# Splitting the second layer of the second chunk into float16 halves in a top-k attention and two-MLP kernel

## The chip, the cores and the metric

The kernel runs on one core of one Trainium2 chip. The metric is the time of one execution on the device in microseconds (us); lower is better. The median of three runs before the change is 1272.48 us.

## The reference, cut to what matters

```python
scores = q @ k.T / sqrt(64)                 # 4 batches, 8 heads, 576 x 576
attn   = softmax(where(scores >= 32nd largest of the row, scores, -1e9))
x = attn @ v                                # 2304 tokens x 512
x = (sigmoid(x @ w_gate) * (x @ w_val)) @ w_out          # 512 -> 1536 -> 512
out = relu(x @ w_in)**2 @ w_out2                         # 512 -> 2048 -> 512
```

The weights arrive as 64-bit numbers, q, k and v as float32.

## The kernel before, in words

Tokens are worked on in blocks of 128. The list `CHUNKS` (L28) makes them into twelve chunks: six of one block, then six of two. A chunk goes through attention first: for each of its blocks and each of eight heads one "unit" takes the scores (`sp`, TensorE), copies them to SBUF (`S`, ScalarE), finds the 32nd largest number of each row with four MAX8 and three MATCH_REPLACE (VectorE, L389 and L396), makes the softmax, transposes it and multiplies it with the values. Then the chunk goes through the first layer (gate, value, product, `w_out`) and the second (`w_in`, squared relu, `w_out2`). The weights are called `wg`, `wv`, `wo`, `wi` and `w2`; tiles of `w2` show as `w` in the profile.

There are two ways through the layers. `moe32` (L895) is the plain one, for the two chunks in `PLAIN` (L43): float32 weights (`wi_c` and so on, as converted from 64 bits) against float32 activations. A product of two float32 operands is two matmul instructions. `moe` (L768) is the split one, for all others: each weight is a pair of float16 tiles, a high half and what it leaves (`wi_w`), and so is each activation, and three matmuls (`SPLIT`) stand for one product. The split way needs power-of-two scales: of the weights (`scale`, L629, from a sum of squares on TensorE) and of each chunk's activations (L817 to L829: squares on ScalarE into `x`, their sum on TensorE into `x2pq`, its maximum on VectorE, `x2cm`, two halves on ScalarE and VectorE).

A weight is split by `split` (L653): a cast on ScalarE (L658) and a subtraction, on VectorE for two splits of three (L661) and on GpSimd for the third (`LOP`, L663 and L664). One split covers a pair of 128x512 blocks; there are 34 (6 each of wg, wv, wo, 8 each of wi, w2). A split writes a new tile and then frees the float32 one, so it comes behind the last plain use of that pair. In the kernel before, the main loop lists all splits in `todo` with the step of the second plain chunk at which each is due: a plain chunk has six steps of its first layer and eight of its second, so those of wg, wv and wo fall into its first layer and those of wi and w2 into its second.

Each layer works on two blocks of hidden columns at a time, a pair. In `moe32` one pair is in flight: the products of pair n+1 are issued ahead of the accumulation of pair n. In the split second layer three are (`DEPTH2`).

The program text gives each piece a priority (`at`, `tc.cur_priority`); a scheduler turns these into a fixed order of instructions on each engine. The weights come in over SyncE's queue with the queries, keys and values; SyncE also stores the outputs (`ob`).

Of the kernel before, what the change touches and what calls it, by code (L numbers as in the profile page):

```python
# [43 lines left out]
TD = 0  # L44
# [10 lines left out]
GRAM = {2: ("wg",), 3: ("wv",), 5: ("wo",), 9: ("wi",), 13: ("w2",)}  # L55
# [19 lines left out]
def tile_topk_attention__then__two_moe_layers(  # L75
# [692 lines left out]
    def moe(ci, nxt=None):  # L768

        m = ahead.pop(ci)  # L770
        tts, N, ix, l1_pair = chunks[ci], m.N, m.ix, m.l1_pair
        accs = []

        def l1_acc(fp, gh):
            if not accs:
                for h in range(2):
                    accs.append(ps_a.tile([P, 512], F32, tag="acc", name=f"acc1_{ci}_{h}"))

            last = fp == NF1 // 2 - 1
            for e, d in sorted(  # L780
                ((e, d) for e in range(2) for d in range(KM)),
                key=lambda t: (t[1], t[0]) if last else t,
            ):
                f = 2 * fp + e
                if True:
                    for x, (a, b_) in enumerate(SPLIT):
                        nc.tensor.matmul(  # L787
                            accs[d // 2][:, (d % 2) * N : (d % 2 + 1) * N],
                            wblk("wo", a, f, d * P, P),
                            gh[:, b_, e * N : (e + 1) * N],  # L790
                            start=(f == 0 and x == 0 and d % 2 == 0),
                            stop=(f == NF1 - 1 and x == 2),
                            skip_group_check=True,
                        )

        queue = m.queue
        depth = max(1, len(queue))
        for fp in range(len(queue), NF1 // 2):
            queue.append((fp, l1_pair(fp)))
            yield  # L800
            if len(queue) > depth:
                l1_acc(*queue.pop(0))
        while len(queue) > 1:
            l1_acc(*queue.pop(0))
        if nxt:
            nxt()
        l1_acc(*queue.pop(0))

        pool, kw = (wpool, {"tag": "w"}) if ci >= X2W else (mpool, {"tag": "m4", "bufs": M4})
        x2 = pool.tile([P, 2, KM, N], F16, name=f"x2_{ci}", **kw)  # L810
# [82 lines left out]


    def moe32(ci, xt):  # L895
# [387 lines left out]
```

## Time and profile before

| what | value |
|---|---|
| median of three runs (lowest to highest) | 1272.48 us (1272.18 to 1277.38) |
| the profiled execution: its time, its span | 1270.1 us, 1267.8 us |
| TensorE matmul busy | 1171.9 us, 92% of the span |
| VectorE, ScalarE, GpSimd busy | 956.3, 830.0, 844.9 us (75%, 65%, 67%) |
| chain that ended last | TensorE 62%, VectorE 14%, ScalarE 9%, DMA 7%, GpSimd 5% |

The span runs from the first to the last instruction of the profiled execution; its time includes what lies around it. A matmul's record lasts longer than the step from one to the next, since matmuls overlap; the pace is read from the chain, which merges those that follow each other. In the rows below PE is TensorE, PEld its weight loads, DVE VectorE, ACT ScalarE, POOL GpSimd and SPq SyncE's queue.

### The profile page before, as it was taken

The page shows a single profiled execution, that of the slowest core. Times are in us where ns is not written, and L with a number is a line of the kernel's source. Part 1 is how long each engine was busy: PE and PEld are TensorE (multiplying, and loading weights), DVE is VectorE, ACT ScalarE, POOL GpSimd, SP SyncE. Part 2 cuts the span into 40 slices and gives each one's busy share as a digit, 9 for nine tenths or more (in the row PEclk, how much of TensorE's full clock was granted, in tenths as well). Part 3 has the DMA queues.
Part 4 walks back from the last instruction along what each step waited for, and adds up shares of the span by engine and source line. Part 5 has one row for each costly group of instructions (what it writes and reads, how often), then busy time and mean ns, then how long its engine had stood idle before and what let it go on. Part 6 is the DMA issues. An engine that isn't in the chain of part 4 may idle for free.

```text
span 1267.8 us, 30670 instructions
## 1 busy us (share of the span) xinstructions
PE 1171.9 (92%) x11477; PEld 952.5 (75%) x11477; DVE 956.3 (75%) x1965; ACT 830.0 (65%) x1719; POOL 844.9 (67%) x1294
## 2 busy tenths in 40 slices
PE   6657889999889989899998999999999999999998
PEld 5436877987777868779786778877886887787775
DVE  6998789899789868889997788998999969210010
ACT  4998996577676766667766676776676757322122
POOL 1788774488776576777875887797688749515223
PEclk9667999999989999999997999999999999999999
DMA  6988763223354346665667465466544623200000
GB/s 183 366 293 284 259 191 85 57 78 88 109 151 118 95 93 147 147 134 119 146 128 155 99 164 120 119 138 154 105 101 92 126 48 67 55 1 1 18 1 17
DMA packets 243188, 153.92 MB, mean 121 GB/s; under 512 B 193120, under 2 KB 209504, under 8 KB 243040
## 3 DMA queue, kind: packets, MB, share of 16 engines
q1 hardware_dynamic: 243040, 151.97, 47.1%
q8 instruction: 90, 1.47, 0.5%
q14 instruction: 58, 0.48, 0.1%
HBM read 105.51 MB, written 18.09 MB: 97 GB/s over the span
## 4 chain that ended last, share of the span: by engine, by line
PE 62%; DVE 14%; ACT 9%; DMA 7%; POOL 5%; issue 3%; SPq 1%; DVEq 0%; POOLq 0%; ACTq 0%
PE ph L851 11%; PE acc L872 10%; PE pv L747 7%; PE pg L747 7%; PE acc L787 6%; PE sp L374 6%; DVE mx L389 5%; DVE W L396 5%; PE xp L506 2%; PE ph L952 2%; DMA PT<-S 2%; DMA kst<-ks 2%; PE acc L969 2%; PE xp L533 2%; PE qpt L334 1%
## 5 line engine op out<-in xcount | busy, mean ns | idle before, releaser
L389 DVE MAX8 mx<-W 128x8 f32<-128x576 f32 x432 | 327.9, 759 | 11.1
L396 DVE MATCH_REPLACE8 W<-mx,W 128x576 f32<-128x576 f32 x288 | 213.8, 742 | 0.0
L851 PE MATMUL ph<-x,wi_w 128*128 128x256 f16 (+1 forms) x1920 | 190.7, 252 | 4.6 <-ACT x L825 3.6
L872 PE MATMUL acc<-w_w,rh 128*128 128x512 f16 x768 | 181.8, 379 | 2.2 <-POOL rh L864 2.2
L851 PEld LDWEIGHTS <-wi_w 128*128 128x128 f16 x1920 | 156.4, 98 | 30.6 <-issue 5.2
L747 PE MATMUL pv<-xs,wv_w 128*128 128x256 f16 (+1 forms) x1440 | 147.0, 254 | 6.0 <-DVE th L759 4.8
L747 PE MATMUL pg<-xs,wg_w 128*128 128x256 f16 (+1 forms) x1440 | 148.2, 253 | 3.1 <-ACT xs L520 2.2
L374 PE MATMUL sp<-kst,qt 128*128 128x288 f32 x608 | 135.3, 335 | 15.7 <-DMA kst<-ks 8.8
L408 ACT ACTIVATE W<-S,mx 128x576 f32<-128x576 f32 x144 | 111.8, 776 | 51.7 <-DVE mx L389 51.4
L454 POOL TENSOR_TENSOR S<-W,S 128x512 f16<-128x512 f32 x192 | 137.0, 736 | 1.6
L747 PEld LDWEIGHTS <-wv_w 128*128 128x128 f16 x1440 | 117.9, 99 | 22.1 <-issue 9.2
L747 PEld LDWEIGHTS <-wg_w 128*128 128x128 f16 x1440 | 118.6, 99 | 17.4 <-issue 1.0
L377 ACT COPY S<-sp 128x576 f32<-128x576 f32 x144 | 92.0, 639 | 57.3 <-PE sp L374 37.5
L872 PEld LDWEIGHTS <-rh 128*128 128x128 f16 x768 | 72.5, 98 | 74.0 <-POOL rh L864 2.8
L787 PEld LDWEIGHTS <-wo_w 128*128 128x128 f16 x1440 | 117.9, 98 | 12.6 <-issue 0.8
L389 DVE MAX8 mx<-S 128x8 f32<-128x576 f32 x144 | 107.3, 745 | 25.0 <-ACT S L377 25.0
L759 DVE TENSOR_TENSOR th<-pv,th 128x512 f32<-128x512 f32 (+1 forms) x60 | 34.5, 576 | 121.3 <-PE pv L747 113.9
L374 PEld LDWEIGHTS sp<-kst,qt 128*128 128x128 f32 x608 | 92.4, 196 | 27.8 <-DMA kst<-ks 8.0
L452 POOL TENSOR_SCALAR W<-W,rz 128x576 f32<-128x576 f32 x96 | 71.9, 749 | 59.8 <-ACT S L451 57.4
L863 POOL TENSOR_TENSOR r<-r 128x512 f32<-128x512 f32 (+1 forms) x80 | 69.6, 871 | 57.4 <-ACT rh L862 51.8
L451 ACT ACTIVATE S<-W,rz 128x576 f16<-128x576 f32 x96 | 74.2, 774 | 50.4 <-DVE rz L447 47.1
L396 DVE MATCH_REPLACE8 W<-mx,S 128x576 f32<-128x576 f32 x144 | 106.9, 743 | 0.3 <-issue 0.3
(290 smaller groups left out, 2349.6 us busy)
## 6 DMA issues: line engine op xcount, KB each, us to landing
kst<-ks SPq DMA_DIRECT2D x112, 288.0 KB, 3.2
v<-vd SPq DMA_DIRECT2D x32, 320.0 KB, 3.4
qn<-in_q_dram SPq DMA_DIRECT2D x128, 64.0 KB, 2.4
wi_r<-in_moe_w_in_dram SPq DMA_DIRECT2D x16, 512.0 KB, 6.1
w_r<-in_moe_w_out_dram SPq DMA_DIRECT2D x16, 512.0 KB, 4.5
v<-in_v_dram SPq DMA_DIRECT2D x56, 128.0 KB, 2.4
wg_r<-in_moe_w_gate_dram SPq DMA_DIRECT2D x12, 512.0 KB, 6.4
wv_r<-in_moe_w_val_dram SPq DMA_DIRECT2D x12, 512.0 KB, 7.0
```

Of the source, the lines that this page charges most:

```text
L374: nc.tensor.matmul(sp[:, e, 0:HALF], l, r, start=(x == 0), stop=(x == len(ops) - 1))
L377: nc.scalar.copy(ss.rearrange("p (e s) -> p e s", e=2), sp[:, :, 0:HALF])
L389: m8 = nc.vector.max(mx[:, r], cur)
L396: nc.vector.match_replace(wk, mx[:, r], cur, NEG)
L408: nc.scalar.activation(wk, ss, AF.Prelu, bias=kth, scale=-1.0, alpha=1.0 / BIG)
L451: nc.scalar.activation(pp[:, 0:S], wk, AF.Copy, scale=rz)
L452: nc.gpsimd.tensor_scalar(wk, wk, rz, 1.0, op0=ALU.mult, op1=ALU.mult)
L454: nc.gpsimd.tensor_tensor(pp[:, o : o + e - f], wk[:, f:e], pp[:, f:e], op=ALU.subtract)
L747: nc.tensor.matmul(pp[:, e * N : (e + 1) * N], wblk(wd, a, c, f0, P), xs[:, b_, c, :], start=(e == 0 and n == 0), stop=(n == 3 * KM - 1), ...
L787: nc.tensor.matmul(accs[d // 2][:, (d % 2) * N : (d % 2 + 1) * N], wblk("wo", a, f, d * P, P), gh[:, b_, e * N : (e + 1) * N], start=(f == ...
L851: nc.tensor.matmul(ph[:, e * N : (e + 1) * N], wblk("wi", a, c, f0, P), x2[:, b_, c, :], start=(e == 0 and n == 0), stop=(n == 3 * KM - 1) ...
L872: nc.tensor.matmul(acc2[i][:, 0:DM], gh[:, b_, e * N + i * P : e * N + (i + 1) * P], wblk("w2", a, f, 0, DM), start=(f == 0 and x == 0), s ...
```

## The change

The second chunk keeps the plain first layer and takes the split second layer. For that the second half of `moe` becomes a function `second`, which both `moe` and `moe32` call; the second chunk's split activations are written over its own input tile. The splits of wi and w2 are due while the first chunk does its second layer (as soon as all weights have been converted), those of wg, wv and wo in the second chunk's first layer as before. The scales of wi and w2 are taken two steps earlier. The first chunk's plain second layer holds two pairs in flight. Intermediate results of the plain layers are written in place instead of to a second buffer. The second chunk's second layer gets steps of 3 instead of 4 in the priority count.

```diff
-TD = 0
+MIXED = (1,)
+DEPTH1 = (1, 1)
+DEPTHP = 2
+CMS = 3.0
+W2S = 12
...
-GRAM = {2: ("wg",), 3: ("wv",), 5: ("wo",), 9: ("wi",), 13: ("w2",)}
+GRAM = {2: ("wg",), 3: ("wv",), 5: ("wo",), 7: ("wi",), 11: ("w2",)}
...
+    def second(ci, ix, x2, srcs, nxt=None):
...
+        if ix is None:
+
+            nc.vector.scalar_tensor_tensor(
+                us[:, 0:1], iy, float(2.0 ** (2 * TB - 7)), scales["wi"][1], op0=ALU.mult, op1=ALU.mult
+            )
...
+        yield from second(ci, ix, x2, srcs, nxt)
...
-            g = mpool.tile([P, 2 * N], F32, tag="hi", bufs=HIB, name=f"g_{ci}_{fp}")
-            nc.vector.tensor_tensor(g, pg[:, 2 * N : 4 * N], th, op=ALU.mult)
-            return g
+            nc.vector.tensor_tensor(th, pg[:, 2 * N : 4 * N], th, op=ALU.mult)
+            return th
...
+        if ci in MIXED:
+            x2 = xt.rearrange("p d n -> p (d n)").bitcast(F16)
+            h = KM * N // 2
+            yield from second(
+                ci,
+                None,
+                x2.rearrange("p (a c n) -> p a c n", a=2, c=KM),
+                [accs[0][:, i * h : (i + 1) * h].rearrange("p (d n) -> p d n", d=KM // 2) for i in range(2)],
+            )
+            return
...
-            if prev is not None:
-                l2_acc(*prev)
-            prev = (fp, g)
-        l2_acc(*prev)
+            if len(prev) > DEPTHP:
+                l2_acc(*prev.pop(0))
+        for p in prev:
+            l2_acc(*p)
...
+    ends = {n: (len(PLAIN) - 1) * per_chunk for n in ("wg", "wv", "wo")}
+    ends.update({n: (len(PLAIN) - 1 - len(MIXED)) * per_chunk for n in ("wi", "w2")})
...
-        todo.append((n1 + 2 * (i // 2) + 2, "wi", i))
+        todo.append((ends["wi"] + n1 + 2 * (i // 2) + 2, "wi", i))
...
-        todo.append((n1 + i + 3, "w2", i))
-    todo = [(max(t[0], TD), *t[1:]) for t in todo]
+        todo.append((ends["w2"] + max(n1 + i + 2 + DEPTHP, W2S), "w2", i))
...
-                tm += CM
-                if ci == PLAIN[-1]:
+                tm += CM if ci not in MIXED or n <= n1 else CMS
+                if nstep[0] == len(steps):
                     at(tm - SUP)
-                    while todo and todo[0][0] <= n:
+                    while todo and todo[0][0] <= PLAIN.index(ci) * per_chunk + n:
                         split(*todo.pop(0)[1:])
```

The scheduler's order moves with it. Three places follow; a name's first numbers are chunk or block, then head or pair, and the last one only counts tiles.

VectorE late in the first chunk's second layer, softmax of block 2, heads 4 and 5. Before:

```order
L389 MAX mx_2_4_2490<-W_2_4_2489 128x8
L396 MATCH_REPLACE W_2_4_2489<-mx_2_4_2490,W_2_4_2489 128x576
L389 MAX mx_2_4_2490<-W_2_4_2489 128x8
L389 MAX mx_2_5_2568<-S_2_5_2452 128x8
L396 MATCH_REPLACE W_2_5_2567<-mx_2_5_2568,S_2_5_2452 128x576
L389 MAX mx_2_5_2568<-W_2_5_2567 128x8
```

Changed:

```order
L393 MAX mx_2_4_2521<-W_2_4_2520 128x8
L665 SCALAR_TENSOR_TENSOR w2_w0_2254<-w2_c0_1659,w2s_2230,w2_w0_2254 128x1024
L400 MATCH_REPLACE W_2_4_2520<-mx_2_4_2521,W_2_4_2520 128x576
L665 SCALAR_TENSOR_TENSOR w2_w1_2257<-w2_c1_1673,w2s_2230,w2_w1_2257 128x1024
L393 MAX mx_2_4_2521<-W_2_4_2520 128x8
L393 MAX mx_2_5_2602<-S_2_5_2483 128x8
L665 SCALAR_TENSOR_TENSOR w2_w3_2321<-w2_c3_1701,w2s_2230,w2_w3_2321 128x1024
L400 MATCH_REPLACE W_2_5_2601<-mx_2_5_2602,S_2_5_2483 128x576
L665 SCALAR_TENSOR_TENSOR wi_w6_2396<-wi_c6_1631,wis_1930,wi_w6_2396 128x1024
L393 MAX mx_2_5_2602<-W_2_5_2601 128x8
```

Splits of w2 and wi now stand between the steps of the softmax, where there were none.

TensorE between the two layers of the second chunk (`acc1_1` ends its first layer, `ph_1_0` begins its second). Before:

```order
L927 MATMUL acc1_1_2585<-g_1_5_2827,wo_c5_1036 128x128 x8
L374 MATMUL sp_3_4_3109<-kst_3_4_0_3021,qt_3_2_0_3033 128x288
L474 MATMUL tp_3_1_3038<-ident_81,W_3_1_2980 128x128 x4
L492 MATMUL tq_3_0_3045<-ident_81,we_3_0_2918 128x128
L374 MATMUL sp_3_4_3109<-kst_3_4_0_3021,qt_3_2_0_3033 128x288 x3
L952 MATMUL ph_1_0_2939<-x_plain_269,wi_c0_1072 128x128 x2
```

Changed, from the last matmul of the new sum of squares on:

```order
L783 MATMUL x2pq_1_2970<-x_plain_269,ones_86 128x128
L338 MATMUL qpt_3_2_3144<-ident_81,qn_3_2_3027 128x128 x2
L378 MATMUL sp_3_4_3241<-kst_3_4_0_3135,qt_3_2_0_3147 128x288 x4
L478 MATMUL tp_3_1_3152<-ident_81,W_3_1_3052 128x128 x4
L496 MATMUL tq_3_0_3159<-ident_81,we_3_0_2951 128x128
L823 LDWEIGHTS wi_w0_1945
L823 MATMUL ph_1_0_2992<-x_plain_269,wi_w0_1945 128x128
```

The same attention work stands between the layers, with the queries' transposes (`qpt`) more; the sum of squares stands ahead of it, and behind it come weight loads and matmuls of the split `wi`.

VectorE in the third chunk's first layer, softmax of block 4, head 1. Before:

```order
L389 MAX mx_4_1_3721<-W_4_1_3720 128x8
L661 SCALAR_TENSOR_TENSOR w2_w3_3263<-w2_c3_1707,w2s_2361,w2_w3_3263 128x1024
L396 MATCH_REPLACE W_4_1_3720<-mx_4_1_3721,W_4_1_3720 128x576
L389 MAX mx_4_1_3721<-W_4_1_3720 128x8
L661 SCALAR_TENSOR_TENSOR w2_w4_3330<-w2_c4_1719,w2s_2361,w2_w4_3330 128x1024
L396 MATCH_REPLACE W_4_1_3720<-mx_4_1_3721,W_4_1_3720 128x576
L759 TENSOR_TENSOR th_2_2_3970<-pv_2_2_3921,th_2_2_3970 128x256
L389 MAX mx_4_1_3721<-W_4_1_3720 128x8
```

Changed:

```order
L393 MAX mx_4_1_3897<-W_4_1_3896 128x8
L400 MATCH_REPLACE W_4_1_3896<-mx_4_1_3897,W_4_1_3896 128x576
L393 MAX mx_4_1_3897<-W_4_1_3896 128x8
L763 TENSOR_TENSOR th_2_2_4146<-pv_2_2_4097,th_2_2_4146 128x256
L400 MATCH_REPLACE W_4_1_3896<-mx_4_1_3897,W_4_1_3896 128x576
L393 MAX mx_4_1_3897<-W_4_1_3896 128x8
```

The splits that stood ahead of `th_2_2` have gone.

## Rows read from the trace of the kernel before

**Rows 1.** Table of stretches: window, each engine's busy us, TensorE's granted clock, DMA share, GB/s.

```profile
core 0: us, PE busy (x) PEld busy (x) DVE busy (x) ACT busy (x) POOL busy (x), PEclk, DMA share, GB/s
175.00:277.50 102.50, 100.45 (x873) 86.99 (x873) 92.91 (x182) 69.88 (x135) 58.04 (x84) 1.00 0.31 86
277.50:329.00 51.50, 50.52 (x422) 39.97 (x421) 43.78 (x79) 42.45 (x89) 41.74 (x61) 1.00 0.38 109
329.00:363.70 34.70, 27.78 (x422) 26.57 (x419) 29.70 (x58) 23.40 (x53) 26.76 (x41) 0.95 0.36 100
...
450.00:550.00 100.00, 88.99 (x1232) 74.16 (x1230) 75.28 (x172) 65.85 (x162) 75.98 (x139) 1.00 0.57 127
...
700.00:1060.00 360.00, 356.74 (x3457) 282.97 (x3456) 320.43 (x664) 248.04 (x517) 279.56 (x457) 1.00 0.52 114
```

**Rows 2.** Chain of waits, second chunk's plain second layer: start, length, what.

```profile
283.64 1.78 PE ph L952 x16
285.43 1.72 PE acc L969 x4
```

**Rows 3.** Chain of waits, third chunk's split second layer.

```profile
372.16 1.56 PE ph L851 x28
...
378.98 1.29 PE acc L872 x6
```

**Rows 4.** Timeline of TensorE between the third chunk's layers: start, length; idle before.

```profile
362.71 0.27 PE L819 MATMUL x2pq<-x,ones 128*128 128x128 bf16 x2 [1.74 <-ACT x L817]
...
364.24 1.62 PE L374 MATMUL sp<-kst,qt 128*128 128x288 f32 x7 [0.97 <-POOL qt L350]
366.59 0.85 PE L374 MATMUL sp<-kst,qt 128*128 128x288 f32 x2 [0.73 <-ACT S L377]
367.24 1.93 PE L851 MATMUL ph<-x,wi_w 128*128 128x128 f16 x16
```

**Rows 5.** Timeline of TensorE between the fourth chunk's layers.

```profile
443.73 0.40 PE L819 MATMUL x2pq<-x,ones 128*128 128x128 bf16 x4
...
447.36 1.28 PE L851 MATMUL ph<-x,wi_w 128*128 128x128 f16 x20 [1.12 <-ACT x L825]
```

**Rows 6.** Timeline of SyncE's queue: the store of the second chunk's output.

```profile
319.23 0.34 SPq L988 DMA_DIRECT2D out_dram<-ob  x1
```

**Rows 7.** Groups of instructions, 175 to 365 us, ScalarE and GpSimd: busy us, mean ns, idle before.

```profile
L658 ACT ACTIVATE wi_w<-wi_c,wis 128x1024 f16<-128x1024 f32 x8 | 9.2, 1151 | 1.9 <-DVE w_w L661 1.9
...
L664 POOL TENSOR_TENSOR wi_w<-wi_c,wi_w 128x1024 f16<-128x1024 f32 x2 | 4.3, 2132 | 0.0
...
L663 POOL TENSOR_SCALAR wi_c<-wi_c,wis 128x1024 f32<-128x1024 f32 x2 | 2.2, 1122 | 2.0 <-ACT wi_w L658 2.0
```

**Rows 8.** Groups of instructions, 175 to 365 us, VectorE: splits of w2 and wi.

```profile
L661 DVE SCALAR_TENSOR_TENSOR w_w<-w_c,w2s,w_w 128x1024 f16<-128x1024 f32 x5 | 10.1, 2020 | 0.9 <-ACT w_w L658 0.9
...
L661 DVE SCALAR_TENSOR_TENSOR wi_w<-wi_c,wis,wi_w 128x1024 f16<-128x1024 f32 x6 | 8.6, 1435 | 0.1
```

**Rows 9.** Timeline of VectorE in the third chunk's first layer.

```profile
332.85 4.37 DVE L661 SCALAR_TENSOR_TENSOR w_w<-w_c,w2s,w_w 128x1024 f16<-128x1024 f32 x1
...
340.57 0.42 DVE L759 TENSOR_TENSOR th<-pv,th 128x256 f32<-128x256 f32 x1
```

**Rows 10.** Costliest groups of the page, VectorE's softmax steps: busy us, mean ns, idle before.

```profile
L389 DVE MAX8 mx<-W 128x8 f32<-128x576 f32 x432 | 327.9, 759 | 11.1
L396 DVE MATCH_REPLACE8 W<-mx,W 128x576 f32<-128x576 f32 x288 | 213.8, 742 | 0.0
```

**Rows 11.** Timeline of TensorE in the third chunk's first layer.

```profile
334.78 1.50 PE L747 MATMUL pg<-xs,wg_w 128*128 128x128 f16 x24
341.04 2.57 PE L747 MATMUL pv<-xs,wv_w 128*128 128x128 f16 x24 [4.75 <-DVE th L759]
```

**Rows 12.** Timeline of GpSimd there, the first and last of seven in a row.

```profile
331.41 0.70 POOL L225 TENSOR_SCALAR vm<-vm,vsc 128x512 f32<-128x512 f32 x1
...
334.98 1.15 POOL L711 TENSOR_TENSOR xs<-xt,xs 128x512 f16<-128x512 f32 x1
```

**Rows 13.** Table of stretches, right behind TensorE's wait.

```profile
341.10:343.40 2.30, 2.30 (x24) 2.30 (x24) 2.23 (x5) 1.89 (x8) 2.12 (x4) 0.53 0.11 35
```

More of the change, by code (lines that the diff above doesn't have):

```diff
@@ L766, in moe_head @@
         m.N, m.ix, m.l1_pair = N, ix, l1_pair
[L768 to L810, printed above, removed]
+    def second(ci, ix, x2, srcs, nxt=None):
+        tts = chunks[ci]
+        N = len(tts) * P
         KH = KM // 2
-        srcs = [a[:, 0 : KH * N].rearrange("p (d n) -> p d n", d=KH) for a in accs]
         with tc.high_priority(offset=XUP):
@@ L892, in moe, with l1_acc @@
         yield
+    def moe(ci, nxt=None):
+        m = ahead.pop(ci)
+        tts, N, ix, l1_pair = chunks[ci], m.N, m.ix, m.l1_pair
+        accs = []
+        def l1_acc(fp, gh):
+            if not accs:
+                for h in range(2):
+                    accs.append(ps_a.tile([P, 512], F32, tag="acc", name=f"acc1_{ci}_{h}"))
+            last = fp == NF1 // 2 - 1
+            for e, d in sorted(
+                ((e, d) for e in range(2) for d in range(KM)),
+                key=lambda t: (t[1], t[0]) if last else t,
+            ):
+                f = 2 * fp + e
+                if True:
+                    for x, (a, b_) in enumerate(SPLIT):
+                        nc.tensor.matmul(
+                            accs[d // 2][:, (d % 2) * N : (d % 2 + 1) * N],
+                            wblk("wo", a, f, d * P, P),
+                            gh[:, b_, e * N : (e + 1) * N],
+                            start=(f == 0 and x == 0 and d % 2 == 0),
+                            stop=(f == NF1 - 1 and x == 2),
+                            skip_group_check=True,
+                        )
+        queue = m.queue
+        depth = max(1, len(queue))
+        for fp in range(len(queue), NF1 // 2):
+            queue.append((fp, l1_pair(fp)))
+            yield
+            if len(queue) > depth:
+                l1_acc(*queue.pop(0))
+        while len(queue) > 1:
+            l1_acc(*queue.pop(0))
+        if nxt:
+            nxt()
+        l1_acc(*queue.pop(0))
+        pool, kw = (wpool, {"tag": "w"}) if ci >= X2W else (mpool, {"tag": "m4", "bufs": M4})
+        x2 = pool.tile([P, 2, KM, N], F16, name=f"x2_{ci}", **kw)
+        KH = KM // 2
+        srcs = [a[:, 0 : KH * N].rearrange("p (d n) -> p d n", d=KH) for a in accs]
+        yield from second(ci, ix, x2, srcs, nxt)
     def moe32(ci, xt):
@@ L961, in l2_pair @@
             nc.scalar.activation(r, ph[:, 0 : 2 * N], AF.Relu)
-            g = mpool.tile([P, 2 * N], F32, tag="hi", bufs=HIB, name=f"rr_{ci}_{fp}")
-            nc.gpsimd.tensor_tensor(g, r, r, op=ALU.mult)
-            return g
+            nc.gpsimd.tensor_tensor(r, r, r, op=ALU.mult)
+            return r
         def l2_acc(fp, g):
@@ L975, in l2_acc @@
                 )
-        prev = None
+        prev = []
         for fp in range(NF2 // 2):
-            g = l2_pair(fp)
+            prev.append((fp, l2_pair(fp)))
             yield
-            if prev is not None:
-                l2_acc(*prev)
-            prev = (fp, g)
-        l2_acc(*prev)
+            if len(prev) > DEPTHP:
+                l2_acc(*prev.pop(0))
+        for p in prev:
+            l2_acc(*p)
         tt = chunks[ci][0]
@@ L1149, in layer2_scales @@
             usc.append(u)
-        return usc[0], scales["w2"][1]
+        return usc[0]
     att = attention()
```

22 lines of the change are left out of this document (13 added, 9 removed).

## The prediction, made before the change was run

> **What bounds the kernel now.** I read the table of stretches first, then the timelines inside them, then the chain of waits for the pace of single operations. The edits act between 175 us, where the first chunk turns from its first to its second layer, and 363.7 us, where the third chunk does; the stretches are cut at the places where the second chunk does so (277.5 us) and where the third has done two pairs (329 us). The reader is to see three different limits [rows 1]. In stage A (175 to 277.5) TensorE is busy 100.45 of 102.50 us and VectorE 92.91: TensorE is full, but VectorE has only 9.6 us to spare. In stage B (277.5 to 329) TensorE is busy 50.52 of 51.50, VectorE 43.78: TensorE alone. In stage C (329 to 363.7) neither is full: TensorE 27.78 of 34.70. Later TensorE leaves 11 of 100 us free between 450 and 550 us, and 3.3 of 360 between 700 and 1060: from there on it runs almost without a gap, so microseconds won before stay won unless the 450 to 550 us stretch eats them.
>
> **Second layer of the second chunk (stage B).** Removed are 128 float32 matmuls of 128 columns and 32 of 512 (two instructions for each of 64 and 16 products). In the chain 16 of the first kind took 1.78 us and 4 of the second 1.72 [rows 2], so 111 ns and 430 ns each: 14.2 + 13.8 = 28.0 us. Added are 192 float16 matmuls of 128 columns and 48 of 512. The third chunk runs the same ones now: 28 took 1.56 us and 6 took 1.29 [rows 3], so 56 and 215 ns: 10.7 + 10.3 = 21.0, with four of the norm (56 ns each, 0.2) 21.2. **TensorE saves 6.8 us**, on the path, since stage B is TensorE's.
>
> Against that stands a new wait. The plain second layer only copied its input; the split one must square it, sum it on TensorE, find a power of two on VectorE, and write two halves. The third chunk shows this at the same width: from the first matmul of the sum at 362.71 to the first product at 367.24 us, with waits of 1.74, 0.97 and 0.73 us in and ahead of it [rows 4], 3.4 us idle. The fourth chunk shows it better covered: from 443.73 to 447.36 with 1.12 us idle [rows 5]. In the new order the queries, scores and a transpose of the attention stand between the sum and the first product, as in the third chunk, so I take 2.5 us, between ends of 1.1 and 3.4. **Stage B: -6.8 + 2.5 = -4.3 us.**
>
> The other engines there: per pair ScalarE gets a square and GpSimd a subtraction more, eight times, work that the third chunk hides today; their splits leave the stage. On SyncE's queue the store of the second chunk's output moves ahead of three key loads of later units that used to stand ahead of it. It is one issue of 0.34 us [rows 6], but if the output is late, those loads stand behind it. I cost it at nothing, since the layer that ends in it is shorter.
>
> **The splits go to stage A.** Each of the 34 splits is one ScalarE cast, 1.15 us, and a subtraction, on VectorE for two of three and on GpSimd for the third (2.13 us after a scaling of 1.12) [rows 7]. The order now has 20 VectorE splits ahead of the second chunk's second layer where it had 10, then three in stage B (it had eight) and none in stage C (it had five). Half a unit of softmax less stands ahead of that point (26.5 units instead of 27). The price of a VectorE split is uncertain: the six of wi took 1.435 us in the mean, the five of w2 2.02, a single one of them 4.37 [rows 8, 9]. Without that one these eleven come to (6 x 1.435 + 5 x 2.02 - 4.37) / 10 = 1.43 us. Ten more cost 14.3; half a unit (two MAX8 of 0.76, one and a half MATCH_REPLACE of 0.74 [rows 10]) gives 2.6 back. That is 11.7 us against 9.6 us of spare VectorE. **Stage A: +2.1 us.** If enough of it slips in beside full TensorE it is 0; at 2.02 us a split with all the spare time used it is +8.0. ScalarE gets 15 more casts (17.3 us on 69.88 of 102.5 busy) and GpSimd five more pairs (16.3 on 58.04) [rows 1]: both still fit.
>
> **Stage C loses its stall.** TensorE stood idle for 4.75 us ahead of 341.04, for VectorE's `th` of the pair before [rows 11]. VectorE was late because the split of w2 that began at 332.85 took 4.37 us [rows 9], while GpSimd ran without a pause from 331.41 to 336.1 [rows 12]. With no split left here that goes. After the stall the granted clock was 0.53 of full, about the lower level of 1.2 GHz [rows 13], and the next 24 matmuls took 2.57 us where 24 had taken 1.50 before it [rows 11]: another 1.1. What is late next is the norm of the third chunk (its 3.4 us stay). **Stage C: -4.75 - 1.1 = -5.9 us.**
>
> The Trainium skill ("SBUF — State Buffer", section "SBUF: two separate sides") says that a VectorE instruction with two SBUF inputs and a GpSimd instruction that reads SBUF take a shared port pair in turn, each for its whole length. The 4.37 us beside GpSimd's run agrees. The page speaks against this change: in stage A GpSimd goes from 58 to 74 us of work, and more splits would meet it. By the splits' row without the long one the sum stays what it is below; by the page, with every new split meeting GpSimd, it would be that of rival 2.
>
> **Two pairs in flight, one buffer instead of two.** In the first chunk's plain second layer TensorE has no idle time worth a row (stage A is full at 100.45 of 102.50). I cost the deeper queue and the in-place writes at nothing; what hides the latency is the attention's matmuls. Wherever VectorE makes those late, the extra pair is what TensorE has left. The scales of wi and w2 come one and two units of softmax earlier, same work.
>
> **Sum.** +2.1 - 4.3 - 5.9 = -8.1 us. The profiled execution took 1270.1 us, so it would take 1262.0; the median of the runs shown is 1272.48, 2.4 higher, so the forecast is **1264.4 us**. At 363.7 us both orders have done the same number of softmax units, and the work behind it is the same, so I add nothing. The ends: A 0, B -5.7, C -5.9 gives 1260.9; A +8.0, B -3.4, C -4.75 gives 1272.3.
>
> **Rivals.**
> (1) VectorE starves TensorE in stage A: none of the 9.6 us of spare time can be used, because VectorE's idle moments come from waiting for scores. Then A is +11.7, the sum +1.5, the time 1274. For it: two engines at 98 and 91% in one stage. Against it: in stage A the old order already used such moments for ten splits.
> (2) The slower side: the same, with every one of the ten new splits held up by GpSimd as the w2 splits were, 2.02 us each. A is then 20.2 - 2.6 = +17.6, the sum +7.4, the time 1279.9. It is slower by over 0.5% from 1.92 us a split on, if no spare time is used. For it: GpSimd's third of the splits moves to the same place, and GpSimd's subtraction takes 2.13 us, longer than a free split. Against it: between them GpSimd was idle for 44 of 102.5 us. The rule of the page above is the mechanism of this rival.
> (3) The gain is given back between 450 and 550 us, where transfers and VectorE already leave TensorE idle for 11 us [rows 1]: half of it gone is 1268.5. Against it: those waits hang on earlier engine work, which comes earlier too.
> (4) The change doesn't do what it says: the split layer doesn't run at 56 ns a matmul because each wait leaves TensorE at the low clock. 24 matmuls in 2.57 us are 107 ns; a fifth of the layer at that pace with the full wait of 3.4 is some 3 us less gain, 1267.
> (5) Better: the third chunk's norm wait also shrinks by 3.4 us with ScalarE freed of splits, and A costs nothing: 1264.4 - 2.1 - 3.4 = 1258.9 or a little less.
>
> **How the numbers follow.** Forecast with its own range of 1260 to 1268: 0.56. Rival 1: 0.12; 2: 0.09; 3: 0.12; 4: 0.05; 5: 0.06. A measurement of this kernel tells about 0.5% from no change, so faster means below 1266.1 and slower above 1278.8. Faster: most of the forecast (0.48) and rival 5: 0.54. Slower: the larger part of rival 2, 0.07. The rest, 0.39, is within. The range of 1257 to 1274 leaves out rival 2, part of rival 1 and a little beyond rival 5.
>
> **What would show it.** Right: the float16 second layer of the second chunk within some 21 us of TensorE's own time; no VectorE split after the second chunk's second layer has begun but three; no wait of TensorE above 2 us in the third chunk's first layer; the second chunk's second layer beginning within a few microseconds of 277.5. Wrong: TensorE idle for transposes or scores before 277 us (rivals 1 and 2, told apart by the mean of VectorE's splits there); a longer 450 to 550 us stretch (3); low granted clock in the split layer (4).

## The result: 1282.3 us, slower

The changed kernel takes **1282.32 us** in the median (1279.54 to 1283.14), the kernel before 1273.76 beside it: ratio **1.0065, interval 1.0048 to 1.0082**, so 0.65% more. The forecast was 1264.4, with a range of 1257 to 1274. Rival 2 (VectorE's splits held up by GpSimd) had 1279.9.

The profiled execution of the changed kernel took 1283.14 us (span 1281.4). Its table of stretches, to be read beside [rows 1]; the second chunk's norm is at 288.4 us now (before, its second layer began at 277.5), the third chunk's at 368.7 (363.7):

```profile
core 0: us, PE busy (x) PEld busy (x) DVE busy (x) ACT busy (x) POOL busy (x), PEclk, DMA share, GB/s
175.00:222.00 47.00, 45.06 (x402) 36.74 (x403) 44.43 (x89) 36.25 (x71) 28.98 (x40) 1.00 0.43 120
222.00:255.00 33.00, 25.42 (x177) 21.83 (x177) 30.43 (x41) 23.61 (x36) 30.91 (x27) 0.90 0.18 53
255.00:288.40 33.40, 32.14 (x293) 30.16 (x291) 31.87 (x54) 26.14 (x46) 25.84 (x27) 1.00 0.23 62
175.00:288.40 113.40, 102.62 (x868) 88.73 (x868) 106.73 (x182) 86.00 (x151) 85.73 (x94) 0.97 0.30 83
288.40:339.00 50.60, 46.35 (x517) 37.09 (x518) 42.37 (x92) 36.27 (x92) 33.73 (x63) 0.97 0.35 96
339.00:368.70 29.70, 26.33 (x408) 24.61 (x406) 19.03 (x50) 16.22 (x41) 17.69 (x36) 1.00 0.45 125
...
368.70:1281.40 912.70, 871.98 (x8965) 697.68 (x8964) 646.88 (x1391) 545.39 (x1178) 597.03 (x990) 0.99 0.43 98
```

Stage A takes 113.4 us instead of 102.5 (+10.9), B and C together 80.3 instead of 86.2 (-5.9). TensorE's idle time in A is 10.8 us (2.0 before). Most of the loss sits in one third of A, from 222 to 255 us: TensorE busy 25.42 of 33 at a clock of 0.90, and GpSimd, which the prediction counted as having room, busy 30.91 (16.64 in the same window before). In A as a whole GpSimd has 85.73 us instead of 58.04.

The wait itself, on TensorE, and behind it the second chunk's norm:

```profile
249.90 3.79 PE L945 MATMUL acc<-th,wo_c 128*128 128x128 f32 x16 [7.29 <-DVE th L935]
...
283.84 2.05 PE L945 MATMUL acc<-th,wo_c 128*128 128x128 f32 x16
...
287.24 0.55 PE L783 MATMUL x2pq<-x_plain,ones 128*128 128x128 bf16 x4 [0.67 <-ACT x_plain L781]
...
290.07 0.40 PE L378 MATMUL sp<-kst,qt 128*128 128x288 f32 x1 [1.76 <-ACT qt L350]
291.59 0.66 PE L378 MATMUL sp<-kst,qt 128*128 128x288 f32 x3 [1.12 <-POOL qt L354]
292.70 1.12 PE L478 MATMUL tp<-ident,W 128*128 128x128 f32 x4 [0.45 <-POOL W L442]
```

After 7.29 us of idling the granted clock is 0.50, the lower level of 1.2 GHz (249.90 to 253.50 us), and the next 16 float32 matmuls take 3.79 us where 16 of the same take 2.05 later (283.84): another 1.7 us. Why `th` was late stands in the timelines of VectorE, GpSimd and ScalarE (start, length, what, idle before):

```profile
243.88 1.90 DVE L665 SCALAR_TENSOR_TENSOR wv_w<-wv_c,wvs,wv_w 128x1024 f16<-128x1024 f32 x1 [1.92 <-ACT wv_w L662]
...
246.44 3.06 DVE L665 SCALAR_TENSOR_TENSOR wg_w<-wg_c,wgs,wg_w 128x1024 f16<-128x1024 f32 x1
249.43 0.41 DVE L935 TENSOR_TENSOR th<-pg,th 128x256 f32<-128x256 f32 x1
```

```profile
235.02 2.14 POOL L668 TENSOR_TENSOR w_w<-w_c,w_w 128x1024 f16<-128x1024 f32 x1
237.14 2.15 POOL L667 TENSOR_SCALAR wi_c<-wi_c,wis 128x1024 f32<-128x1024 f32 x1
239.38 1.06 POOL L432 TENSOR_SCALAR bs<-bs 128x1 f32<-128x1 f32 x1
240.53 2.14 POOL L668 TENSOR_TENSOR wi_w<-wi_c,wi_w 128x1024 f16<-128x1024 f32 x1
...
244.69 1.27 POOL L409 TENSOR_SCALAR bs<-mx 128x1 f32<-128x1 f32 x1
245.93 0.40 POOL L934 TENSOR_SCALAR th<-th 128x256 f32<-128x256 f32 x1
246.30 2.12 POOL L668 TENSOR_TENSOR wg_w<-wg_c,wg_w 128x1024 f16<-128x1024 f32 x1
```

```profile
242.70 1.15 ACT L662 ACTIVATE wv_w<-wv_c,wvs 128x1024 f16<-128x1024 f32 x1 [2.62 <-POOL wi_w L668]
...
244.22 0.39 ACT L933 ACTIVATE th<-pg 128x256 f32<-128x256 f32 x1
```

Read it backwards. VectorE's `th` (249.43) stood behind a split that took 3.06 us and ended 1.08 us after GpSimd's own subtraction (246.30 to 248.42); the shortest splits of the stage take 1.26. GpSimd had made its part of that `th` ready at 246.33, behind an instruction on a single column (`bs`, 128x1) that took 1.27 us. ScalarE's part (244.22) and the split before (243.88) stood behind a cast that, by the trace, waited until 242.70 for GpSimd's subtraction of wi. From 231 to 254 us GpSimd had no pause above 0.1 us; its subtraction of wi had followed on a scaling of 2.15 us, instead of the 1.12 of [rows 7], and on another single column of 1.06.

### The profile page after: what moved, and what is told of

Its sections match the earlier page's. It is cut to its first block, busy times and chain, and to the rows that moved or that the text cites. A ratio compares the mean times of both kernels' runs of the same rounds, so it can differ in the third digit from the quotient of the medians.

```text
span 1281.4 us, 30909 instructions
## 1 busy us (share of the span) xinstructions
PE 1172.7 (92%) x11561; PEld 952.7 (74%) x11561; DVE 957.1 (75%) x1973; ACT 831.5 (65%) x1730; POOL 850.7 (66%) x1302
## 4 chain that ended last, share of the span: by engine, by line
PE 52%; DVE 19%; DMA 8%; POOL 6%; ACT 6%; issue 5%; SPq 3%; DVEq 0%; POOLq 0%; ACTq 0%
PE ph L823 12%; PE acc L844 10%; DVE mx L393 8%; DVE W L400 7%; PE pv L751 5%; PE pg L751 5%; PE acc L885 5%; PE sp L378 4%; DMA PT<-S 2%; PE xp L510 2%; PE xp L537 2%; PE pg L924 1%; DMA kn<-in_k_dram 1%; PE ph L980 1%; PE acc L945 1%
## 5 line engine op out<-in xcount | busy, mean ns | idle before, releaser
L823 PE MATMUL ph<-x,wi_w 128*128 128x256 f16 (+1 forms) x1920 | 194.0, 255 | 3.9 <-ACT x L789 2.6
L823 PEld LDWEIGHTS <-wi_w 128*128 128x128 f16 x2112 | 170.3, 99 | 33.4 <-issue 6.3
L844 PE MATMUL acc<-w_w,rh 128*128 128x512 f16 x816 | 194.0, 380 | 0.9 <-POOL rh L836 0.8
L378 PE MATMUL sp<-kst,qt 128*128 128x288 f32 x608 | 133.1, 332 | 10.4 <-DMA kst<-ks 4.6
L844 PEld LDWEIGHTS <-rh 128*128 128x128 f16 x816 | 76.9, 98 | 77.4 <-POOL rh L836 1.7
L835 POOL TENSOR_TENSOR r<-r 128x512 f32<-128x512 f32 (+1 forms) x88 | 74.9, 851 | 59.2 <-ACT rh L834 58.2
```

The costliest lines, as they stand in the source:

```text
L378: nc.tensor.matmul(sp[:, e, 0:HALF], l, r, start=(x == 0), stop=(x == len(ops) - 1))
L823: nc.tensor.matmul(ph[:, e * N : (e + 1) * N], wblk("wi", a, c, f0, P), x2[:, b_, c, :], start=(e == 0 and n == 0), stop=(n == 3 * KM - 1) ...
L835: nc.gpsimd.tensor_tensor(r, r, r, op=ALU.mult)
L844: nc.tensor.matmul(acc2[i][:, 0:DM], gh[:, b_, e * N + i * P : e * N + (i + 1) * P], wblk("w2", a, f, 0, DM), start=(f == 0 and x == 0), s ...
```

## The experiments

Ratios are to the kernel before, run beside each. "Idle" is TensorE's idle time from 175 us to the second chunk's norm, and from there to the third's (before and e1, with no norm there, cut at 277.5 us; before: 2.0 and 7.9; changed: 10.8 and 7.6). "Units" is how many softmax units stand ahead of the third chunk's norm in VectorE's order (before and changed: 36.2); a run with more of them has done more by then.

| run | median, ratio (interval) | idle, us | units |
|---|---|---|---|
| e1 rest alone | 1271.4, 0.9971 (0.9947 to 0.9996) | 2.1, 5.2 | 36.2 |
| e2 without GpSimd's five | 1267.9, 0.9932 (0.9909 to 0.9955) | 2.5, 6.8 | 36.2 |
| e4 without VectorE's eleven | 1270.2, 0.9972 (0.9947 to 0.9997) | 6.9, 5.6 | 36.5 |
| e6 without all sixteen | 1274.9, 1.0004 (0.9982 to 1.0025) | 4.8, 9.5 | 37.2 |
| e13 one-input passes | 1282.5, 1.0069 (1.0047 to 1.0092) | 9.6, 5.9 | 36.2 |
| e16 MAX8 | 1275.5, 1.0014 (1.0001 to 1.0027) | 8.0, 6.6 | 37.2 |
| e17 MAX8 in place | 1275.0, 1.0011 (0.9994 to 1.0029) | 5.2, 7.5 | 37.2 |
| e18 scaling on ScalarE | 1278.9, 1.0043 (1.0026 to 1.0059) | 4.0, 6.8 | 35.2 |
| e5 five to VectorE | 1278.6, 1.0038 (1.0019 to 1.0057) | 5.8, 8.9 | 35.8 |
| e7 all on VectorE | 1278.0, 1.0030 (1.0012 to 1.0047) | 2.8, 8.1 | 35.2 |
| e3 spread | 1280.6, 1.0035 (1.0009 to 1.0061) | 7.6, 7.8 | 37.2 |
| e8 wg, wv later | 1289.3, 1.0118 (1.0087 to 1.0148) | 7.3, 14.2 | 38.2 |
| e9 w2 in time | 1287.9, 1.0103 (1.0070 to 1.0136) | 6.1, 15.3 | 37.8 |
| e10 all in time | 1301.1, 1.0207 (1.0169 to 1.0245) | 3.6, 28.2 | 37.5 |
| e11 two pairs first | 1280.3, 1.0043 (1.0024 to 1.0062) | 12.2, 7.5 | 35.8 |
| e12 both | 1275.6, 1.0011 (0.9992 to 1.0029) | 3.4, 7.9 | 36.2 |
| e14 e12, first 17 on VectorE | 1281.2, 1.0055 (1.0035 to 1.0075) | 1.8, 10.4 | 35.2 |
| e15 e12, all on VectorE | 1287.5, 1.0113 (1.0087 to 1.0140) | 1.1, 11.9 | 35.2 |

### Is it the splits, and whose?

**e1**: two pairs in flight, in-place buffers, early scales; no split second layer.

```diff
-MIXED = (1,)
+MIXED = ()
```

> The second chunk keeps its plain second layer and all splits keep their old due times; what is left of the change is two pairs in flight, one buffer instead of two, and the earlier scales of wi and w2. Crowding (the loss comes from the splits moved into the first chunk's second layer and the second chunk's first): within 3 us of the kernel before (1273.8), softmax unit 24 within 2 us of the old time. The rest is to blame: above 1278, unit 24 late by 10 us or more.

It takes no more than the kernel before, rather less. What the prediction costed at nothing costs nothing; the loss belongs to the split layer and its splits. Of the versions that keep every low half it alone is quicker than both kernels, by 0.3% of the kernel before.

**e2, e4, e6**: the low halves of wi and w2 that GpSimd makes (five), that VectorE makes (eleven), or all sixteen are left out; the high half is used in their place.

```diff
+        if name in ("wi", "w2") and nsp[0] % LOP == 0:   # e4: nsp[0] % LOP; e6: no condition
+            nolow.add(id(t))
-        if not (LOP and nsp[0] % LOP == 0 and nsp[0] > LOA):
+        elif nsp[0] % LOP:
```

> The changed kernel, where the five low halves of wi and w2 that GpSimd makes are left out (the high half is used in their place); VectorE's eleven stay. Two engines that hold each other up: the splits that stay fall from 1.3 to 3.2 us each to about 1.3, TensorE's 7.3 us wait ahead of 250 us goes, unit 24 is late by less than 8 us against 17.9 in the changed kernel, the time 1270 to 1275. VectorE's own load alone: the splits of VectorE stay long, unit 24 late by 14 us or more, the time 1279 or more.

> The changed kernel, where the eleven low halves of wi and w2 that VectorE makes are left out (the high half is used in their place); GpSimd's five stay. Any theory in which VectorE's splits are the loss: unit 24 within 4 us of the old time, the time 1262 to 1269, which is the gain of the split layer and of the third chunk without its price. If the split layer, its norm or the reordering further on is the loss: still above 1275.

> The changed kernel with all sixteen low halves of wi and w2 left out (the high half is used in their place), the fourth corner beside all (norm of the second chunk at 288.4 us), VectorE's alone (276.8) and GpSimd's alone (284.6). If the two costs only add up, it comes at 273 us (284.6 + 276.8 - 288.4). If a part of the loss is there only when both engines split, it comes later than 274.5, nearer to 276.8. In both cases the time is 1262 to 1269.

e2 comes out 0.68% under the kernel before (8.7 us by the ratio, 6.8 by the medians), close to the forecast's 8.1, with all twenty of VectorE's splits still ahead of the norm. The order on VectorE hardly moved, the stretch from 222 to 255 us is full again, and the splits of wi and w2 take their undisturbed time (means 1277 and 1333 ns, against 1383 and 1923 in the changed kernel):

```profile
222.00:255.00 33.00, 32.67 (x260) 28.91 (x260) 32.39 (x46) 29.10 (x44) 23.52 (x26) 1.00 0.19 53
```

```profile
L668 DVE SCALAR_TENSOR_TENSOR w_w<-w_c,w2s,w_w 128x1024 f16<-128x1024 f32 x6 | 8.0, 1333 | 0.1
...
L668 DVE SCALAR_TENSOR_TENSOR wi_w<-wi_c,wis,wi_w 128x1024 f16<-128x1024 f32 x5 | 6.4, 1277 | 0.4 <-ACT wi_w L663 0.4
```

So VectorE's twenty splits by themselves are no loss (rival 1 falls). The time of e2 is better than the 1270 to 1275 expected. e4 takes most of the loss away too (1.2 us above its range), though GpSimd is as busy from 222 to 255 us as in the changed kernel:

```profile
222.00:255.00 33.00, 33.00 (x266) 29.45 (x265) 23.92 (x39) 28.16 (x44) 30.81 (x31) 1.00 0.19 54
```

GpSimd's load by itself is no loss either. Both runs were some 10 us late at unit 24 all the same, which no theory had: softmax and layers trade places, and units are a poor gauge inside the stage. e6 missed its range by far: with less work than either it was slower than e2 and no quicker than e4. Its order differs (one more softmax unit ahead of the third norm), and it idles 9.5 us between the norms. In stage A its longest wait (3.08 us, ahead of 245.62) is of the kind seen above, as both engines still split wg and wv: GpSimd's subtraction is held up, and its part of `th` stands behind it.

```profile
241.28 1.46 DVE L668 SCALAR_TENSOR_TENSOR wg_w<-wg_c,wgs,wg_w 128x1024 f16<-128x1024 f32 x1
245.13 0.42 DVE L940 TENSOR_TENSOR th<-pg,th 128x256 f32<-128x256 f32 x1 [2.39 <-POOL th L939]
...
241.75 2.97 POOL L671 TENSOR_TENSOR wg_w<-wg_c,wg_w 128x1024 f16<-128x1024 f32 x1
```

Shares of the loss can therefore not be added up from these four runs; e2 against the changed kernel, where the order stays, is the firm one.

### Load, or holding each other up?

**e13, e16, e17** replace each of VectorE's eleven subtractions by something of about its length that was meant to let GpSimd alone: two one-input passes; one MAX8; one MAX8 tied to the cast. Low halves left out or doubled as the expectations say; e17's maxima also overwrite eight columns of the high half.

```diff
-            nc.vector.scalar_tensor_tensor(t[:, 1], c, s, t[:, 0], op0=ALU.mult, op1=ALU.subtract)
+            nc.vector.tensor_scalar(t[:, 1], c, s, 1.0, op0=ALU.mult, op1=ALU.mult)   # e13: twice
+            nc.vector.max(out=m8, in_=c.rearrange("p e f -> p (e f)"))                # e16
+            nc.vector.max(out=t[:, 0, 0, 0:8], in_=c.rearrange("p e f -> p (e f)"))   # e17
```

> The changed kernel, where each of the eleven VectorE subtractions for wi and w2 (two inputs in SBUF, 1.27 us when nothing holds it up) is replaced by two passes with one input each over the same tile (0.68 us each at the shortest rows of that shape); the low half of those is then a second high half. VectorE's load and GpSimd's load are as in the changed kernel. If the loss is in the way in which two-input VectorE instructions and GpSimd hold each other up: GpSimd's subtractions of wi at 2.14 us instead of 3.12, TensorE's idle time from 175 us to the second chunk's norm 2 to 6 us instead of 10.8, the time 1266 to 1275. If the load of the two engines is enough: idle above 9 us, 1279 to 1285.

> The changed kernel, where each of VectorE's eleven subtractions for wi and w2 is replaced by a MAX8 over the same raw tile: one input, about 1.25 us by the 0.76 us of a MAX8 over 576 columns, and of a kind that the trace nowhere shows held up by GpSimd (the passes of the run before were: 0.73 us at the shortest, up to 2.6). The low halves of those splits are left out (the high half is used in their place). VectorE's load then is about that of the changed kernel with undisturbed splits, GpSimd's is the same; the second chunk's norm stands half a softmax unit later in the order, some 3 us. If the two engines holding each other up is the loss: GpSimd's subtractions of wi at 2.14 us, TensorE's idle time from 175 us to the norm below 7 us (6.9 without those eleven at all), the time 1268 to 1274. If the load is: idle 9 us or more, 1279 or more.

> The run before with the same MAX8 in the place of each of VectorE's eleven subtractions for wi and w2, but now tied to the ScalarE cast as the subtraction is (it writes its eight maxima over the first columns of the cast's output), so that it stands where the split stood, from 197 us on; without that tie most of them had slipped ahead of 197 us. The low halves are left out. Holding each other up as the loss: the eleven take 1.2 us each, GpSimd's subtractions of wi 2.14, TensorE's idle time from 175 us to the norm below 8 us with one softmax unit more in it, the time 1269 to 1276. Load as the loss: idle of 10 us or more, the time 1279 or more.

By its ranges e13 fell on the side of load (1282.5 us, 9.6 us idle). It didn't separate the theories, though: its passes were themselves held up, so that VectorE's load rose (25.1 us for the 22 passes, 18.4 for the eleven splits). Minimum, median and longest of a pass, in ns:

```profile
L666 DVE TENSOR_SCALAR w_w<-w_c,w2s x12: 730/1021/2622, 224.7 to 254.0; 128x1024 f16<-128x1024 f32 x12
L666 DVE TENSOR_SCALAR wi_w<-wi_c,wis x10: 734/753/1898, 198.2 to 235.5; 128x1024 f16<-128x1024 f32 x10
```

e16's instructions slipped ahead of 197 us, out of the crowd; it proves nothing either. e17 keeps them in place. MAX8 takes the same time in all eleven cases, nine of them with GpSimd at work beside it for more than 1 us, and GpSimd's subtractions of wi take it too (2136 to 2146 ns, where the changed kernel had up to 3132):

```profile
L667 DVE MAX8 w_w<-w_c x6: 1207/1208/1216, 225.0 to 246.6; 128x8 f16<-128x1024 f32 x6
L667 DVE MAX8 wi_w<-wi_c x5: 1209/1217/1228, 199.2 to 231.1; 128x8 f16<-128x1024 f32 x5
L672 POOL TENSOR_TENSOR wi_w<-wi_c,wi_w x3: 2136/2142/2146, 204.4 to 235.3; 128x1024 f16<-128x1024 f32 x3
```

```profile
222.00:255.00 33.00, 30.16 (x225) 26.15 (x225) 31.24 (x48) 29.47 (x48) 30.24 (x31) 0.96 0.20 56
```

VectorE (31.24) and GpSimd (30.24) are as busy between 222 and 255 us as in the changed kernel (30.43 and 30.91), but TensorE gets 225 matmuls done there instead of 177. The ratio falls from 1.0065 to 1.0011, some 7 us of the loss; idle time below 8 and time below 1276, as holding each other up wanted. Load as the whole cause falls. The 7 us are no clean share, since here too, as in e6, one softmax unit more stands ahead of the third norm; the window's row is the firmer sign. And e4, without those eleven at all, is another 5 us quicker: beside GpSimd's work, VectorE's load counts too.

**e18, e5, e7** take GpSimd's share another way.

```diff
-            nc.gpsimd.tensor_scalar(c, c, s, 1.0, op0=ALU.mult, op1=ALU.mult)
+            nc.scalar.activation(c, c, AF.Copy, scale=s)     # e18
-LOA = 0
+LOA = 17     # e5
-LOP = 3
+LOP = 0      # e7
```

> The changed kernel, but the scaling that GpSimd does ahead of each of its eleven subtractions (1.12 us) is done by ScalarE, so that GpSimd's share of a split falls from 3.26 to 2.14 us; ScalarE, 86.6 us busy of the 113.4 from 175 us to the norm, gets some 9 more. If GpSimd's time in the crowd is the loss: half to two thirds of it goes, 1273 to 1279. If ScalarE's own queue, which casts one split after another as buffers come free, takes its place: 1280 or more.

> The changed kernel, but the first 17 splits are all made by VectorE: six of the eleven low halves that GpSimd made stay with it, all but one of those of wi and w2 go. GpSimd as the loss (its queue, or the time in which it and VectorE hold each other up): the splits take about 1.3 us each on VectorE, five more of them cost at most 6.5 us, the norm between the second chunk's layers comes 276 to 283 us (288.4 in the changed kernel, 276.8 without GpSimd's five), the time 1266 to 1273. VectorE's load as the loss: the norm at 288 us or later, the time 1280 or more.

> The changed kernel with all 34 low halves on VectorE and none on GpSimd. Holding each other up as the whole loss: nothing holds VectorE up any more, 1.27 us a split, the time 1266 to 1274. VectorE's load counts too: 30 splits or so ahead of the second chunk's second layer, 13 us more than with half of GpSimd's taken over, of which the most shows in the norm's time: 285 us or later, the time 1274 to 1284.

e18 gives 2.8 us back, a third of the loss, at the slow end of its first range. e5 and e7 missed what holding-up alone would give. In e7 a split on VectorE takes 1.31 us in the mean, hardly held up, and TensorE is full from 222 to 255 us. But 31 splits stand in a stretch where VectorE was 91% busy (e5: 25 of 1.45), so the softmax falls behind (e7: some 23.5 units done ahead of the second chunk's norm, changed: 26.5). 3 to 5 us are gained on the changed kernel, no more. GpSimd's share can't just be handed over.

### Can the splits go elsewhere?

**e3, e8**: scales and splits of wg and wv later (e3 also wi and w2 earlier). **e9, e10**: w2's splits, or w2's and wi's, due just ahead of their use. **e11**: two pairs in flight in the second chunk's first layer (wo's splits come a step later with it). **e12**: e9 and e11. **e14, e15**: e12 with the first 17, or all, splits on VectorE.

```diff
+GRAM = {2: ("wi",), 5: ("wo",), 7: ("w2",), 18: ("wg",), 19: ("wv",)}   # e3; wg, wv due 6 steps later
+GRAM = {5: ("wo",), 7: ("wi",), 11: ("w2",), 18: ("wg",), 19: ("wv",)}  # e8; wg, wv due 6 steps later
+        todo.append((per_chunk + n1 + i, "w2", i))                      # e9, e10, e12, e14, e15
+        todo.append((per_chunk + n1 + 2 * (i // 2) - 2, "wi", i))       # e10
+DEPTH1 = (1, 2)                                                         # e11, e12, e14, e15
```

> The changed kernel with the scales and the splits of wg and wv due during the second chunk's second layer, so that 14 VectorE splits instead of 20 stand ahead of it and eight behind its start, and with the scales of wi and w2 earlier (steps 2 and 7 instead of 7 and 11). Crowding: unit 24 late by less than 8 us, the second chunk's second layer some 3 us slower than in the changed kernel, the time 1268 to 1276. If the number of splits in the two plain chunks is what counts and not how they bunch: 1280 or more.

> The changed kernel with the scales and splits of wg and wv due in the second chunk's second layer, those of wi, w2 and wo as in the changed kernel (the spread version before also asked for wi and w2 earlier, and was 16 us late by unit 20 already). Crowding between 222 and 289 us: unit 24 late by less than 9 us, and the eight VectorE splits moved cost less in the second layer, where TensorE is done sooner: the time 1268 to 1277. If they cost the same wherever they go: 1280 or more.

> The changed kernel, but w2's eight splits are due only a step ahead of the pairs of the second chunk's second layer that use them; wi's stay in the first chunk. Ahead of the norm VectorE now has 16 splits instead of 20, behind it seven before the third chunk's first th instead of three. If the loss is the crowd of splits between 222 and 289 us: TensorE's idle time from 175 us to the norm falls from 10.8 to below 6 us, the norm of the third chunk comes no later than 365 us at one and a half softmax units more, the time 1264 to 1273. If the loss is in the split layer's norm and in ScalarE's and GpSimd's work on it: above 1278.

> The changed kernel, where wi's splits too are due only two steps ahead of the pairs that use them: nearly the old places of all splits, beside the split layer. If the splits moved are the loss: TensorE's idle time from 175 us to the norm falls to some 3 us (2.0 before), and what stays is the split layer's gain of 6.8 us less its norm wait of 4, the time 1266 to 1273. If the split layer must now wait for its own splits, TensorE loses the gain inside it: 1273 to 1280. If the splits are not the loss: 1280 or more.

> The changed kernel with two pairs in flight in the second chunk's first layer too, so that TensorE has a pair's products to do while th stands behind the splits on VectorE. If TensorE's 7.3 us wait ahead of 249.9 us is a loss of its own: it falls below 3 us, the time 1274 to 1279. If VectorE is the limit of the whole stretch, the wait turns up at the next scores or transposes: within 2 us of the changed kernel, 1280 to 1284.

> Both together: w2's splits due a step ahead of their use and two pairs in flight in the second chunk's first layer. If both are losses of their own it is the quickest of the four, 1262 to 1270; if one covers for the other, within 2 us of the better one of the two.

> The run with w2's splits in time and two pairs in flight (1275.6), and the first 17 splits all on VectorE. If GpSimd's share of the splits is still a loss there: 1268 to 1273. If that run has no crowd left: within 3 us of it.

> The same with all 34 splits on VectorE. If GpSimd and VectorE holding each other up is what is left of the loss: 1265 to 1272. If VectorE's load is: 1277 or more.

Moving splits behind the norm eases stage A (TensorE idle for 7.3, 6.1 and 3.6 us in e8, e9 and e10, of 10.8) and pays for it in the split layer (14.2, 15.3 and 28.2, of 7.6). Inside it e10's TensorE waits for the layer's own casts and splits:

```profile
298.62 0.40 PE L823 MATMUL ph<-x_plain,wi_w 128*128 128x128 f16 x2 [5.15 <-ACT wi_w L662]
...
344.28 4.24 PE L823 MATMUL ph<-x_plain,wi_w 128*128 128x128 f16 x38 [3.03 <-POOL wi_w L668]
```

e3 lost 16 us by its twentieth unit already; in the code an early scale of wi asks for all weights up to wi first. It says nothing on the crowd; e8 leaves that part out. e8 and e9 came out in the slower of their ranges. e10's 1301.1 us lies where the splits were not to be the loss (1280 or more), but its waits are those of the theory that had 1273 to 1280: right in kind, over 20 us short in size. e11 kept the wait (7.39 us), now ahead of the next pair's `pg`, which the trace has wait for the same `th`: alone, the deeper queue doesn't help. Together with w2 in time, though, 222 to 255 us is full (TensorE 33.00 of 33.00 in e12), and e12 gives back 7 of the changed kernel's 8 us; still 6 us above the range in which each edit cures a loss of its own. Why the two together do what neither does alone is not settled. e14 and e15 were slower than e12, e15 as far as VectorE's load as the rest of the loss would have it (1277 or more): TensorE's idle time between the norms rose from 7.9 to 10.4 and 11.9 us, with one softmax unit less done.

## Why the prediction was wrong

**Stage A (+2.1 forecast, +10.9 measured) is the step that failed**, at the words that GpSimd's five more pairs, 16.3 us on 58.04, "still fit". GpSimd went up by 27.7 us. The five pairs of wi and w2 took 20.8 us instead of 16.3:

```profile
L668 POOL TENSOR_TENSOR wi_w<-wi_c,wi_w 128x1024 f16<-128x1024 f32 x3 | 8.4, 2798 | 0.1
L667 POOL TENSOR_SCALAR wi_c<-wi_c,wis 128x1024 f32<-128x1024 f32 x3 | 4.4, 1471 | 3.5 <-ACT PT L479 3.4
L668 POOL TENSOR_TENSOR w_w<-w_c,w_w 128x1024 f16<-128x1024 f32 x2 | 4.3, 2134 | 0.1
L667 POOL TENSOR_SCALAR w_c<-w_c,w2s 128x1024 f32<-128x1024 f32 x2 | 3.7, 1861 | 2.4 <-ACT w_w L662 2.4
```

In e4, without VectorE's splits of wi and w2, the same ten take their undisturbed 2.14 and 1.12 us. A sixth pair (wo) now lies inside the stage, 3.3 us, and the thirteen `bs<-mx` of a single column take 4.5 us more. And GpSimd's idle time was spread over the stage, while the new splits all fall between 197 and 260 us, since the scale of w2 is there only from 223 us. An engine's sum over 100 us said nothing on these 33.

The price of a VectorE split was the second fault. The twenty of stage A took 34.4 us (1.72 each):

```profile
L665 DVE SCALAR_TENSOR_TENSOR w_w<-w_c,w2s,w_w 128x1024 f16<-128x1024 f32 x6 | 11.5, 1923 | 0.4 <-PE acc L996 0.4
L665 DVE SCALAR_TENSOR_TENSOR wg_w<-wg_c,wgs,wg_w 128x1024 f16<-128x1024 f32 x3 | 7.0, 2345 | 0.0
L665 DVE SCALAR_TENSOR_TENSOR wi_w<-wi_c,wis,wi_w 128x1024 f16<-128x1024 f32 x5 | 6.9, 1383 | 0.4 <-ACT wi_w L662 0.4
L665 DVE SCALAR_TENSOR_TENSOR wv_w<-wv_c,wvs,wv_w 128x1024 f16<-128x1024 f32 x4 | 6.5, 1624 | 1.9 <-ACT wv_w L662 1.9
L665 DVE SCALAR_TENSOR_TENSOR wo_w<-wo_c,wos,wo_w 128x1024 f16<-128x1024 f32 x2 | 2.5, 1265 | 0.0
```

The ten of the kernel before took 16.5 us there by the same view (6.6 for wo, 5.4 for wv, 4.5 for wg), 1.65 each. I had taken the price from wi and w2 in stages B and C ([rows 8]) and struck out the longest; stage A's own rows were at hand and higher. Still, VectorE's excess alone would not have broken the forecast: e2 runs the same twenty.

**Rival 2 named the mechanism**, and its 1279.9 us is 2.4 short of the result; it got 0.09. That the number is so close is partly luck: the rival had A at +17.6 (measured +10.9) and B and C at -10.2 (-5.9). The rule of the Trainium skill ("SBUF — State Buffer", section "SBUF: two separate sides") on the port pair that the two engines take in turn is borne out by the rows: VectorE's 3.06 us split ended 1.08 us after GpSimd's subtraction had. What the rival lacked was the way back: GpSimd is held up as well, and the softmax, the gates and the casts that wait for a buffer stand in its queue.

**Stages B and C (-10.2 forecast, -5.9 measured).** The matmul saving is there: in the chain

```profile
302.64 1.56 PE ph L823 x28
...
311.24 1.29 PE acc L844 x6
```

the same paces as [rows 3]. C's stall of 4.75 us [rows 11] is gone as forecast: no wait of TensorE above 1.4 us from 302 to 365 us. The norm cost 4.0 us of waiting (0.67 + 1.76 + 1.12 + 0.45), beyond its upper end of 3.4, and 1.5 us more through the lower clock behind it (granted 0.50 from 292.2 to 295.6 us). 3.2 us of other waits were left, so that idle time between the norms hardly fell (7.9 to 7.6). From 175 us to the third chunk's norm the terms are: -6.8 of matmuls, +8.4 idle (10.0 to 18.4), +2.1 of lower clock (half of TensorE's busy time at the lower level, 3.4 and 7.7 us). Together that is +3.7 against a measured +5.0; 1.3 us are not accounted for.

**Behind it** I had added nothing. By the medians some 3.5 of the 8.5 us arise there. By the profiles it is 8.6, but the profiled execution of before was 3.7 us under its median. Rival 3 had the gain given back between 450 and 550 us, and these two executions don't show that. Two rows of the changed kernel, then one of before; the last two run from the third chunk's norm to the seventh's, with 47.0 and 47.25 softmax units in them:

```profile
450.00:550.00 100.00, 88.76 (x1202) 74.70 (x1202) 79.42 (x186) 66.81 (x164) 71.90 (x133) 0.98 0.60 130
368.70:692.00 323.30, 298.45 (x3752) 250.65 (x3751) 278.94 (x622) 224.19 (x530) 227.46 (x424) 0.98 0.56 129
...
363.70:687.70 324.00, 300.03 (x3749) 252.22 (x3750) 279.62 (x619) 224.56 (x528) 229.27 (x424) 0.97 0.56 128
```

TensorE's idle time between 450 and 550 us is 11.2 us (11.0 before), and up to the seventh norm nothing is lost. What the profiled execution loses behind stage C it loses from there on: 589.4 us instead of 580.0, TensorE idle for 15.8 instead of 9.9, in good part in waits for loads of keys. The other runs' profiled executions took 580 to 586 us there. No run tells whether that is more than chance.

**The parts at nothing** (depth, in-place buffer, scales) were right by e1; the moved store was not tried apart. Of rival 4 the 1.5 us behind the norm are left, as the paces in the chain are full from 302 us on; its sum was too low besides (a fifth of 21.0 us at 107 instead of 56 ns is 3.8 us, with 0.9 of wait 4.7 and not 3). Rival 5 falls with stage A.

## What to carry to other kernels

Before work is moved to an earlier stage, price it in the window of a few tens of microseconds in which it can start (here from the scale's arrival on), for every engine it runs on, and with that window's own durations. Work that two engines can only do in turn must be counted on both, and the in-order queues behind it with it. And a split that a layer uses must be ready before the layer: moved into it, it cost more (1.0207) than in front of it.

## What the runs showed of the hardware that was not expected

A one-input VectorE pass over 128x1024 float32 takes 0.73 us at its shortest and up to 2.62 in e13, so one input is no protection. The Trainium skill ("SBUF — State Buffer", section "SBUF: two separate sides") counts VectorE instructions in a two-port performance mode among the holders of the pair; e13 agrees if its passes run in one, for which their pace alone speaks (0.73 us where MAX8 takes 1.21 over the same tile). MAX8 was never held up (eleven of eleven in e17, 1207 to 1228 ns, nine of them beside GpSimd). On GpSimd the hold-up shows most in its smallest instructions, those of a single column; in stage A, before and changed:

```profile
L405 POOL TENSOR_SCALAR bs<-mx 128x1 f32<-128x1 f32 x13 | 4.0, 304 | 6.5 <-DVE mx L389 6.3 <-DVE x_2s L133 0.2
L409 POOL TENSOR_SCALAR bs<-mx 128x1 f32<-128x1 f32 x13 | 8.5, 652 | 3.5 <-DVE mx L393 3.5
```

All six instructions on one column (`bs`) that took more than 1 us in stage A of the changed kernel ended 0.07 to 0.17 us after the end of a split on VectorE.
